# One core, a delta-rule recurrence and a GELU MLP: the written order of all five instruction queues is replaced by another

## The chip, the cores and the metric

The kernel runs on one core of a Trainium2 chip. The time is the device time of one execution in microseconds (us), the median of three runs. The core has five engines that the text names as the profile does: PE (matrix products; PEld is its weight load), DVE, ACT and POOL (elementwise work), and SP, which here only issues DMA transfers. Each engine works off its own queue in order.

## The reference

Four batches of eight heads run a delta-rule recurrence over 768 tokens with a 48 x 48 state; its output, 3072 tokens of 384 numbers, goes through an MLP with the tanh form of GELU.

```python
k_n = k / (np.linalg.norm(k, axis=-1, keepdims=True) + 1e-06)
for t in range(S):
    y[:, :, t] = np.einsum('bhd,bhde->bhe', q[:, :, t], state)
    v_old = np.einsum('bhde,bhd->bhe', state, kt)
    state = state + bt[:, :, :, None] * np.einsum('bhd,bhe->bhde', kt, vt - v_old)
...
h = x @ w_in
g = 0.5 * h * (1.0 + np.tanh(c * (h + 0.044715 * h * h * h)))
return g @ w_out
```

Here B, H, S, D are 4, 8, 768, 48, w_in is 384 x 2048 and w_out 2048 x 384. Inputs and output are float32; the kernel's products are in bfloat16.

## The kernel before

The 768 steps are cut into 12 chunks of 64 tokens. A chunk has 32 heads in all (batch and head); they are worked on as two units of 16 heads, so there are 24 units: chunk c has the units 2c and 2c+1. Two heads share the 128 partitions. Within a chunk the recurrence is solved as a triangular system, so that only a 48 x 48 state passes from chunk to chunk.

The names in the order are operation, dot, chunk or unit. For a chunk c: k, q, v load it (four DMA issues each; the k of chunk 0 comes in two halves, k0x0 and k0x1, of four issues each). sq, sum, pow, eps, inv make 1/norm of k. For a unit u: kn and qb write normalized k and q in bfloat16 (tile tok); T (for the first four units Tk and Tq) transposes them on PE and kT (kTk, kTq) copies them out of PSUM, or one DMA, turn, does both; G (GD, GQ) are the products of k with k and with q; dn copies the first and wq masks the second on DVE, or wqa on ACT with wqb on POOL. vb casts v.

For a chunk, leaf: F folds dn, lp multiplies by beta, x0 begins a recursion inside blocks of 8 tokens, L spreads lp, and twelve short DVE steps xm1, xa1 to xm6, xa6 run the recursion, each on the one before. xb multiplies by beta. For a unit: xe spreads xb into a tile zt of 128 x 1024, KZ is a product with it, kz its copy, GM two products, lw their masked copy (128 x 1024), and X10, X11 build the start of the inverse in tile bd. Two rounds refine it: A4, rt4, B4, then two copies into bd (bde40 and bde41 straight from PSUM, or xi4 on ACT or DVE and bdc40, bdc41 on POOL or DVE), and the same with 5 for 4.

For a chunk, chain: V and K form the right side from v and the state, R copies it, U solves with bd, Un copies, S makes the state's step and Sn adds it, Q and O make the output, On copies it, X with xT (or one DMA, turnx) transposes it. The MLP of a chunk is sixteen up products of three matmuls (up0 to up15, 128 x 256, line 780), four gelu on ACT of 1024 columns (line 784), eight down products of four matmuls (down00 to down13, 128 x 384, line 791), two copies Z0, Z1 and the output's DMA. Every chunk's MLP needs its own chain, and every chain needs the state of the chunk before; everything ahead of V does not.

At the start there are presets: constants by memset, copy and affine select on DVE and POOL (ident, sel, rows, blk, own, mlw, muq, tmpl and others; bdz, pad, tri and ladj preset tiles that are later only partly written), beta's load, transposes (betaT) and spreading (betaS, betaC), and warm_up (line 419), products of a zero tile wz with itself, 128 x 512, whose results nobody reads.

The weights W1 (w_in) and W2 (w_out) come in two transfers each (w1.0, w1.1, w2.0, w2.1 at lines 477 and 479), issued on POOL's queue. w1 waits for the loads of k of chunk 1, w2 for those of v of chunk 0.

No scheduler runs when the kernel is built. ORDER is one long text, found beforehand, with each operation's engine (a ACT, d DVE, g POOL, s SP, none PE) and, after an @, its PSUM bank of eight. Flow.order puts the operations into the five queues in this order and checks that each stands behind what it needs; Flow.emit adds the semaphore waits. An operation that ORDER leaves out is not done: so it picks between the two ways of a choice (turn or T, wq or wqa and wqb, xi with bdc or bde, turnx or X) and how many zero products run. POOL's work on the upper 64 partitions waits for that on the lower and the other way about. Where a wait stands, the whole queue behind it stands too; DMA issues wait in the same queue as the engine's other work.

## Time and profile before

| | us |
|---|---|
| three runs | 262.83, 263.09, 263.68 |
| median | 263.09 |
| the profiled execution, its own time | 262.76 |
| its span, first to last instruction | 261.0 |

The span is what the profile's rows add up to; the profiled execution's own time is 1.8 us above it. In rows of a timeline the first number is the start and the second the length, both in us from the span's start; in brackets stands the engine's idle time just before and what ended it. Rows of the busy time by stage begin with the stage. SPq, POOLq and ACTq are DMA issues. In the chain of waits each row is a start, a length and what the end of the program waited for at that time. PEclk is the granted clock as a share of full speed. The DMA share is the mean busy share of 16 DMA engines and can pass 1 where packets overlap. In the page's last part the last number is the median us from a DMA's issue to its landing.

### The profile page before, as it was taken

The numbers are of one execution on the slowest core, as the hardware profiler recorded it, in microseconds if no ns is written. First come the engines' busy times: TensorE is split into PE (matmuls) and PEld (weight loads), VectorE is DVE, ScalarE is ACT, GpSimd is POOL, SyncE is SP. The second block draws the span as 40 slices with busy tenths as digits, with TensorE's granted clock in tenths as the row PEclk, the third lists the DMA queues.
The fourth block names the chain that finished last, engine by engine and source line by source line (L and its number), as shares of the span: only waits on it lengthen the run. The fifth ranks groups of instructions, "written<-read, shape, count | busy, mean of one in ns | idle before, by whom it ended". The sixth has DMA issues, their size and how long they took to land.

```text
span 261.0 us, 11939 instructions
## 1 busy us (share of the span) xinstructions
PE 236.6 (91%) x5320; PEld 182.3 (70%) x5320; DVE 191.2 (73%) x444; ACT 169.5 (65%) x261; POOL 135.7 (52%) x172
## 2 busy tenths in 40 slices
...
GB/s 97 162 173 197 123 148 199 127 128 141 133 114 144 124 153 57 122 125 110 162 119 140 108 36 118 159 37 135 130 76 3 4 154 32 31 36 48 45 93 60
DMA packets 104019, 28.10 MB, mean 108 GB/s; under 512 B 98080, under 2 KB 103200, under 8 KB 103968
## 3 DMA queue, kind: packets, MB, share of 16 engines
q1 hardware_dynamic: 98736, 23.56, 51.4%
...
q10 hardware_dynamic: 2352, 0.64, 1.3%
...
HBM read 20.64 MB, written 4.72 MB: 97 GB/s over the span
## 4 chain that ended last, share of the span: by engine, by line
PE 62%; DVE 12%; DMA 10%; SPq 6%; POOL 4%; ACT 3%; issue 2%; POOLq 0%
PE ps L780 20%; PE ps L791 20%; DMA qraw<-in_q_dram 8%; SPq L468 6%; PE ps L660 6%; DVE lw L600 2%; PE ps L597 2%; PE ps L586 2%; PE ps L708 2%; PE ps L546 2%; DMA kraw<-in_k_dram 2%; PE ps L610 1%; PE ps L729 1%; PE ps L522 1%; PE ps L715 1%
## 5 line engine op out<-in xcount | busy, mean ns | idle before, releaser
L780 PE MATMUL ps<-xT,W 128*128 128x256 bf16 x576 | 75.6, 274 | 1.6 <-issue 0.8
L791 PE MATMUL ps<-W,gT 128*128 128x384 bf16 x384 | 72.3, 326 | 0.0
L784 ACT ACTIVATE gT<-ps 128x1024 bf16<-128x1024 f32 x48 | 48.3, 1020 | 22.0 <-PE ps L780 21.7
L780 PEld LDWEIGHTS ps<-xT,W 128*128 128x128 bf16 x576 | 51.7, 98 | 10.7 <-issue 1.2
L791 PEld LDWEIGHTS ps<-W,gT 128*128 128x128 bf16 x384 | 34.1, 97 | 18.6
L678 POOL COPY bd<-xi 64x256 f32<-64x256 f32 x28 | 11.0, 398 | 49.3 <-ACT xi L341 43.5
L600 DVE CAST_PREDICATED lw<-mlw,ps 128x1024 bf16<-128x1024 uint16 x24 | 29.1, 1218 | 7.6 <-PE ps L597 7.4
L650 POOL TENSOR_SCALAR_AFFINE_SELECT bd<-lw 64x512 bf16<-64x512 bf16 x33 | 22.3, 678 | 21.4 <-DVE lw L600 16.0
L494 POOL TENSOR_TENSOR nrm<-nrm,half 128x16 f32<-128x16 f32 x10 | 29.4, 2943 | 4.5 <-DVE nrm L492 4.3
L666 DVE TENSOR_TENSOR rl<-ps,two 128x384 bf16<-128x384 f32 (+1 forms) x48 | 22.8, 486 | 10.6 <-PE ps L660 10.4
L660 PE MATMUL ps<-rl,bd 128*128 128x64 bf16 x384 | 19.5, 198 | 0.7 <-DVE rl L666 0.7
L344 ACT ACTIVATE bd<-ps,low 128x512 bf16<-128x512 f32 x27 | 18.3, 677 | 2.3 <-DVE bd L341 2.3
L341 ACT ACTIVATE bd<-ps 64x512 bf16<-64x512 f32 x27 | 15.7, 585 | 5.9 <-PE ps L660 5.7
L632 DVE TENSOR_TENSOR ps<-ps,xl 128x96 f32<-128x96 f32 (+2 forms) x72 | 16.0, 223 | 4.0 <-PE ps L626 2.1
L660 PEld LDWEIGHTS ps<-rl,bd 128*128 128x128 bf16 x384 | 16.4, 101 | 3.1 <-DVE rl L666 0.9
L522 PE MATMUL ps<-ident,tok 128*128 128x128 bf16 x96 | 10.1, 256 | 8.9 <-POOL tok L513 6.7
L341 DVE COPY ob<-ps 128x384 f32<-128x384 f32 x7 | 3.9, 551 | 19.0 <-PE ps L791 19.0
L660 PEld LDWEIGHTS ps<-lw,bd 128*128 128x128 bf16 x384 | 15.1, 98 | 3.7 <-ACT bd L344 0.5
L635 DVE TENSOR_TENSOR xl<-ps,xl 128x96 bf16<-128x96 f32 (+2 forms) x72 | 16.2, 225 | 1.8
L660 PE MATMUL ps<-lw,bd 128*128 128x32 bf16 (+1 forms) x384 | 17.1, 183 | 0.3 <-ACT bd L344 0.3
L513 POOL TENSOR_TENSOR tok<-kraw,nrm 128x384 bf16<-128x384 f32 x16 | 14.6, 914 | 3.3 <-DVE xl L635 1.1
L341 ACT ACTIVATE dn<-ps 128x512 bf16<-128x512 f32 x20 | 11.9, 594 | 5.7 <-PE ps L546 5.5
(125 smaller groups left out, 437.3 us busy)
## 6 DMA issues: line engine op xcount, KB each, us to landing
...
W<-in_moe_w_in_dram POOLq DMA_DIRECT2D x2, 768.0 KB, 10.5
W<-in_moe_w_out_dram POOLq DMA_DIRECT2D x2, 768.0 KB, 10.8
kraw<-in_k_dram ACTq DMA_DIRECT2D x5, 48.0 KB, 3.3
kT<-tok SPq DMA_TRANSPOSE x12, 3.3
```

The costliest lines, as they stand in the source:

```text
L341: return e.activation(out, in_, ACT.Copy) if e is nc.scalar else e.tensor_copy(out, in_)
L344: return e.activation(out, in_, ACT.Copy, scale=by) if e is nc.scalar else e.tensor_scalar(out, in_, by, None, op0=ALU.mult)
L494: if e is nc.scalar else e.tensor_tensor(nr[:, 1, hx], nr[:, 0, hx], half[:, hx], ALU.pow), reads=[nrn, "half"] + ["one"] * (c < ROOTS),
L600: A(("dve",), op("lw"), lambda e, P: e.copy_predicated(lw[m][:, :, :, :].rearrange("p h w t -> p h (w t)"), mlw[:, :, :].rearrange("p w t ...
L632: A(("dve",), f"xm{m}.{c}", lambda e, P, m=m, w=w, part=part: e.tensor_tensor(part(P), P(f"L.{c}")[:, off[m]:off[m] + 2 * H * w].rearrange ...
L635: A(("dve",), f"xa{m}.{c}", lambda e, P, m=m, part=part: e.tensor_tensor(xl[y][:, :, m + 1:LB], part(P), xl[y][:, :, m + 1:LB], ALU.add), ...
L650: A(("pool", "dve"), op(f"X1{a}"), lambda e, P, src=lw[m][hf(a), :, 1, :], dst=bd[b_][hf(a), :, hf(a)], a=a: e.affine_select(out=dst, in_= ...
L660: ins = e.matmul(P(name)[:, C * h + c0:C * h + c1], bd[b_][:, h, :], rhs[:, h, c0:c1])
L666: A(("dve",), op(f"rt{i}"), lambda e, P, i=i, c0=c0, c1=c1, r_=r_: e.tensor_tensor(r_[:, :, c0:c1], P(ps(f"A{i}")).rearrange("p (h t) -> p ...
L780: ins = e.matmul(P(ph)[:, 256 * f:256 * f + 256].rearrange("p (x t) -> p x t", x=2), W1[:, j, 128 * (i + f):128 * (i + f) + 128], x_[:, :, ...
L784: A(("act",), f"gelu{i // 4}.{c}", lambda e, P, i=i, ph=ph: e.activation(g_[:, i:i + 4, :], P(ph).rearrange("p (f t) -> p f t", f=4), ACT. ...
L791: ins = e.matmul(P(po)[:, 0:DM], g_[:, f, 128 * b:128 * b + 128], W2[:, f, :], start=(f == 0), stop=(f == FC - 1))
```

## The change

ORDER is replaced as a whole, and with it the place of all operations, the engine of many, the PSUM banks, and some choices. The operations' code stays; only the number of zero products that exist to be chosen from goes from 70 to 140. All line numbers move by one (line 780 becomes 781).

What differs between the two orders by count: zero products 8 and 17, the 17 spread in ones and twos over the first 350 of 1668 entries; sel, ident, wz, four of the six bdz and some pads on POOL instead of DVE; k0 loaded wholly by ACT's queue, and beta's part partly by SP's, where k1 now comes first; q0, q1 and q2 issued ahead of v0; the W1 transfers behind the first kn and qb on POOL; the recursions of chunk 0 and 1 woven into each other; transposes of kn and qb by DMA 14 instead of 12, of the output 8 instead of 10; wqa with wqb 12 instead of 10; qb 13 on ACT and 7 on POOL instead of 8 and 12; vb 4 on ACT, 8 on DVE, 12 on POOL instead of 10, 4, 10; X11 12 on DVE and 12 on POOL instead of 4 and 20; X10 8 and 16 instead of 11 and 13; xb 10 on DVE instead of 6. In the new order KZ.4, KZ.5, GM.4, GM.5, A5.3 and B4.3 stand ahead of the first up product, in the old one behind it.

The two orders up to where the first up products stand:

```diff
 ORDER = """
-ident:d tmplz:d tmpl0:g one:g blk1:g tmpl1:g triwq4:g pad4:d wz:d bdz5:d blk2:g ident2:g bdz4:g k0x0.11:s k0x1.10:s k0x0.10:a k0x0.00:a k0x0.01:a
-k1.11:s k0x1.11:s k0x1.00:a k0x1.01:a k1.01:s k1.00:s k1.10:s beta01:a tabS:a beta00:a blk3:g pad5:d ladj5.0:d pad1:d mmlw:d bdz2:d identf:d two:d
-rowz:d rows1:g mln0:g sq.0a:g triwq1:d unit:d bdz3:d ladj4.1:d own:d triwq2:d pad0:d sel:d ladj5.1:d sum.0a:d mwp0:g half:g pow.0a:a trilw2:d trilw3:d
-eps.0a:d inv.0a:d mmuq:d bdz1:g sq.0b:g k2.11:s k2.10:s k2.00:s beta11:a beta10:a kn.0:g fill0@0 fill1@0 fill2@0 fill3@0 fill4@0 fill5@0 fill6@0
-fill7@0 Tk.0@0 betaT0@1 sum.0b:d bdz0:d first1:d pow.0b:a eps.0b:d inv.0b:d kn.1:d Tk.1@2 sq.1:a sum.1:d kTk.0:a pow.1:a GD.0@4 kTk.1:d GD.1@2
-betaT1@0 k2.01:s dn.0:a dn.1:a sq.2:a F.0@2 betaN011:d eps.1:d pad3:d betaN010:d inv.1:d pad2:d betaN000:d betaN001:d kn.2:d kn.3:d sum.2:d Tk.2@3
-q0.01:s q2.00:s q0.00:s q0.10:s q0.11:s v0.00:s q2.10:s q2.11:s v0.10:s q2.01:s v0.11:s k3.10:s k3.01:s v2.10:s v0.01:s lp.0:d betaH0:d L.0@2 x0.0:d
-betaL0:d xm1.0:d betaN101:d xa1.0:d betaN110:d xm2.0:d betaN100:d xa2.0:d xm3.0:d xa3.0:d betaN111:d xm4.0:d Tk.3@1 trilw1:a triwq0:a kTk.2:a GD.2@4
-betaS0@3 kTk.3:a qb.0:a GD.3@6 Tq.0@1 dn.2:a qb.1:a Tq.1@0 betaC0:a dn.3:a betaH1:d xa4.0:d xm5.0:d xa5.0:d kTq.0:a ladj4.0:a kTq.1:a betaL1:d low1:d
-mln1:g w1.1:g trilw0:g first0:g w1.0:g pow.2:g eps.2:g betaS1@3 F.1@6 betaS3@7 xm6.0:d inv.2:d xa6.0:d xb.0:d xe.1:d KZ.1@2 kz.1:a qb.5:a lp.1:d L.1@6
-xe.0:d KZ.0@0 GM.1@4 x0.1:d xm1.1:d xa1.1:d xm2.1:d mwp1:g kn.5:g triwq5:g qb.4:g kn.4:g muq0:g muq1:g low2:g lw.1:d xa2.1:d T.5@2 kz.0:a betaC3:a
-kT.5:a betaC1:a GM.0@0 lw.0:d X10.1:g X11.1:g xm3.1:d xa3.1:d xm4.1:d xa4.1:d X11.0:g X10.0:g betaS2@7 G.5@4 T.4@2 GQ.0@0 A4.1@3 rt4.1:d B4.1@3
-q1.01:s k3.11:s k3.00:s q1.11:s q3.10:s q1.10:s q5.11:s q1.00:s q3.11:s k4.01:s v1.10:s k4.10:s v2.11:s q5.01:s v1.00:s v2.00:s v1.01:s q3.00:s
-k5.11:s v1.11:s k4.11:s k4.00:s q3.01:s dn.5:a betaC2:a wqa.5:a vb.1:a vb.0:a A4.0@7 xm5.1:d xa5.1:d kT.4:d xm6.1:d wq.0:d xa6.1:d rt4.0:d G.4@4
-bde40.1:a bde41.1:a dn.4:a sq.3:a A5.1@3 rt5.1:d B4.0@7 bde40.0:a bde41.0:a w2.1:g xb.1:g xe.3:d wq.4:d sum.3:d xe.2:g B5.1@3 V.0@0 KZ.3@2 F.2@6
-kz.3:a A5.0@7 R.0:a qb.2:a bde50.1:a bde51.1:a lp.2:d GM.3@4 L.2@6 x0.2:d rt5.0:d xm1.2:d xa1.2:d lw.3:d KZ.2@2 GQ.1@0 B5.0@7 xm2.2:d wq.1:d kz.2:a
-bde50.0:a bde51.0:a GM.2@2 w2.0:g pow.3:g eps.3:g xa2.2:d lw.2:d X11.2:g xm3.2:d X10.2:d xa3.2:d xm4.2:d inv.3:d xa4.2:d triwq3:d xm5.2:d xa5.2:d
-xm6.2:d Tq.2@4 U.0@0 qb.3:a kTq.2:a X10.3:g X11.3:g Un.0:a GQ.2@4 Tq.3@7 kTq.3:a O.0@0 On.0:a S.0@2 A4.2@7 Sn.0:a rt4.2:d xa6.2:d X.0@0 xb.2:g xe.5:g
-wq.2:d xT.0:a B4.2@7 GQ.3@2 A4.3@6 up8.0@0 up9.0 xe.4:d rt4.3:d tabG:a xi4.2:a KZ.4@4 kz.4:d B4.3@6 up10.0 up11.0 GM.4@4 wq.3:d lw.4:d X11.4:d
-...
+tmplz:g tmpl0:g one:d blk1:d tmpl1:g wz:g mmuq:g muq0:g mmlw:d pad0:g mln0:g ident:g ident2:g mwp0:g mln1:g bdz0:g triwq3:d bdz1:d ladj5.0:d mwp1:g
+pad3:g pad5:d trilw0:d pad1:d unit:d half:d blk2:g blk3:g rowz:d own:d muq1:g identf:d triwq0:g pad2:g k0x0.11:a k1.11:s k1.10:s beta10:s k0x1.01:a
+k0x1.00:a k0x1.11:a beta11:a q1.01:s q0.10:s k0x1.10:a q0.11:s k1.00:s k1.01:s k0x0.01:a k0x0.10:a q2.10:s k0x0.00:a k2.01:s q2.11:s sq.0b:g beta01:a
+beta00:a tabS:a fill60@0 betaT1@0 sum.0b:d pow.0b:a eps.0b:d sq.1:a inv.0b:d triwq5:d kn.1:d low1:d pad4:d sum.1:d sq.0a:a pow.1:a Tk.1@1 fill79@2
+betaN100:d betaN111:d sum.0a:d eps.1:d inv.1:d betaT0@2 pow.0a:a rows1:g sel:g q0.01:s q0.00:s k2.10:s k2.11:s q1.00:s k2.00:s betaN001:d eps.0a:d
+betaN110:d inv.0a:d betaN011:d betaN000:d betaN101:d betaN010:d betaH0:d q2.01:s q2.00:s kn.2:g Tk.2@3 qb.1:a kTk.2:a kTk.1:a sq.2:a ladj5.1:a kn.0:g
+Tk.0@2 GD.2@4 betaH1:d kn.3:d kTk.0:d dn.2:d bdz4:d Tk.3@3 Tq.1@2 qb.0:g GD.1@0 GD.0@4 betaL0:d sum.2:d betaL1:d dn.0:d kTk.3:a GD.3@6 Tq.0@3 dn.1:a
+dn.3:a F.1@6 F.0@7 kTq.0:d lp.1:d two:d betaS3@3 lp.0:d L.0@7 x0.0:d x0.1:d L.1@6 xm1.0:d xa1.0:d w1.1:g w1.0:g xm1.1:d xm2.0:d first1:g pow.2:g
+eps.2:g first0:g qb.4:g ladj4.0:a kTq.1:a xa2.0:d xa1.1:d xm3.0:d xm2.1:d inv.2:d xa2.1:d xa3.0:d xm3.1:d xm4.0:d xa3.1:d xa4.0:d xm5.0:d xa5.0:d
+betaS0@2 betaC0:a xm4.1:d xm6.0:d xa6.0:d xb.0:d xa4.1:d xm5.1:d xa5.1:d kn.4:g kn.5:g low2:g betaS1@4 qb.5:a betaC3:a triwq4:a q1.11:s v0.00:s
+v1.10:s v0.01:s q1.10:s fill126@5 T.4@5 fill32@3 betaC1:a triwq1:a ladj4.1:d xm6.1:d xa6.1:d xe.0:d xe.1:g xb.1:d kT.4:a v0.10:s v0.11:s fill115@4
+xe.3:d T.5@7 G.4@4 k3.11:s trilw1:a dn.4:a kT.5:a v1.00:s k4.01:s k3.00:s fill98@3 fill74@6 GQ.0@2 wq.0:d KZ.0@6 KZ.1@0 kz.1:a GM.1@0 k4.10:s q3.01:s
+KZ.3@7 fill16@2 xe.2:g lw.1:d X11.1:g triwq2:g qb.2:g kz.0:a q3.00:s G.5@2 wq.4:d trilw3:a kz.3:a dn.5:a qb.3:a tabG:a wqa.5:a GM.0@0 GM.3@6 lw.0:d
+F.2@4 lp.2:d X10.1:d betaS2@5 fill38@0 KZ.2@4 A4.1@0 kz.2:a betaC2:a Tq.3@1 L.2@2 GM.2@4 kTq.3:a x0.2:d lw.3:d xm1.2:d vb.1:d X10.0:g k4.11:s v1.11:s
+k3.01:s k4.00:s q3.11:s k3.10:s bdz2:g X11.0:g vb.0:g trilw2:g A4.0@3 Tq.2@1 fill40@6 kTq.2:a fill127@6 bdz3:g X10.3:g X11.3:g wqb.5:g bdz5:g q3.10:s
+xa1.2:d rt4.1:d B4.1@0 bde40.1:a w2.1:g w2.0:g bde41.1:a xm2.2:d rt4.0:d xa2.2:d lw.2:d fill138@6 fill69@3 B4.0@3 A5.1@0 GQ.1@4 V.0@6 bde40.0:a
+bde41.0:a wqa.1:a A4.3@3 xm3.2:d xa3.2:d xm4.2:d rt5.1:d xa4.2:d xm5.2:d xa5.2:d rt4.3:d fill64@0 A5.0@4 B5.1@5 rt5.0:d xm6.2:d R.0:a bde50.1:a
+v1.01:s v2.00:s v2.01:s v2.11:s q4.01:s v2.10:s k5.01:s k5.10:s X11.2:d X10.2:d xa6.2:d xb.2:d xe.5:d wqb.1:g GQ.2@0 GQ.3@6 B5.0@4 bde51.1:a fill99@3
+wqa.3:a bde50.0:a bde51.0:a A4.2@5 B4.3@2 sq.3:a rt4.2:d xe.4:d KZ.5@3 U.0@6 fill73@5 Un.0:d sum.3:d B4.2@5 fill8@4 kz.5:a xi4.3:a bdc40.3:g bdc41.3:g
+GM.5@2 xi4.2:a bdc40.2:g O.0@6 KZ.4@5 A5.3@4 On.0:a wq.2:d rt5.3:d bdc41.2:d lw.5:d X.0@6 kz.4:a S.0@0 GM.4@4 vb.2:d lw.4:d X11.5:d pow.3:g eps.3:d
+vb.3:d xT.0:a Sn.0:a up8.0@6 up9.0 up10.0 up11.0 gelu2.0:a B5.3@0 up0.0@2 up1.0 up2.0 up3.0 A5.2@1 bde50.3:a qb.7:a gelu0.0:a V.1@6 X11.4:d X10.4:g
+A4.4@4 K.1 rt5.2:d rt4.4:d inv.3:d R.1:a bde51.3:a B5.2@1 bde50.2:d bde51.2:d X10.5:g A4.5@5 rt4.5:d kn.6:d qb.6:g wqb.3:g up4.0@2 B4.4@4 xi4.4:a
+bdc40.4:g up12.0@6 up5.0 up13.0 sq.4:a U.1@0 up14.0 up6.0 up7.0 T.6@5 Un.1:a gelu1.0:a kn.7:g bdc41.4:g Q.1@0 sum.4:d A5.4@4 kT.6:a rt5.4:d O.1 S.1@2
+B4.5@4 up15.0 On.1:d down00.0@5 down01.0 down02.0 gelu3.0:a bde40.5:a bde41.5:a B5.4@6 vb.4:g pow.4:g A5.5@4 down03.0 vb.5:d Sn.1:d rt5.5:d V.2@2
+B5.5@4 bde50.4:a bde51.4:a X.1@6 Z0.0:a xi5.5:a xT.1:d G.6@0 bdc51.5:g K.2 dn.6:a turn.7:s G.7@4 dn.7:a down10.0@6 q4.11:s q4.10:s F.3@7 R.2:a k5.00:s
+...
 """
...
         def warm_up():
-            for i in range(70):
+            for i in range(140):
                 n = f"fill{i}"
                 A(PE, n, lambda e, P, n=n: e.matmul(P(n), wz[:, 0:128], wz[:, :]), reads=["wz"], alloc=(n, 1), frees=[n], mode="m", mm=1)
```

139 lines of the change are left out of this document (67 added, 72 removed).

## The prediction

> **What bounds the kernel now.** I read the page first, then the busy time by stage, then TensorE's timeline and the chain of waits through the stage that is not full.
>
> ```profile
> span 261.0 us, 11939 instructions
> ...
> PE 236.6 (91%) x5320; PEld 182.3 (70%) x5320; DVE 191.2 (73%) x444; ACT 169.5 (65%) x261; POOL 135.7 (52%) x172
> ```
>
> ```profile
> 0.00:11.50 11.50, 3.59 (x8) 1.03 (x8) 10.33 (x30) 1.83 (x5) 9.15 (x21) 0.88 0.75 124
> 11.50:25.60 14.10, 11.78 (x192) 9.58 (x192) 12.71 (x48) 9.79 (x20) 8.39 (x11) 0.50 1.20 185
> 25.60:29.30 3.70, 2.08 (x94) 1.69 (x90) 2.35 (x6) 2.08 (x4) 1.91 (x6) 0.96 0.78 117
> 29.30:49.40 20.10, 16.89 (x403) 13.79 (x400) 16.73 (x42) 16.03 (x29) 13.42 (x16) 0.50 1.01 156
> ...
> 64.30:100.00 35.70, 35.70 (x977) 27.75 (x978) 33.70 (x86) 28.26 (x45) 26.82 (x27) 1.00 0.73 125
> 100.00:240.00 140.00, 137.66 (x3252) 106.79 (x3249) 104.59 (x221) 92.79 (x137) 66.45 (x84) 1.00 0.48 90
> 240.00:257.60 17.60, 17.55 (x132) 12.61 (x129) 0.56 (x1) 7.73 (x10) 0.00 (x0) 1.00 0.25 57
> 257.60:261.00 3.40, 0.00 (x0) 0.00 (x0) 0.00 (x0) 0.47 (x1) 0.00 (x0) 1.00 0.45 116
> ```
>
> The columns after the stage are its length, the busy time of PE, PE's weight loads, DVE, ACT and POOL, then granted clock, DMA share and GB/s. From 64.3 to 257.6 PE is busy 190.9 of 193.3 us: 2.4 us idle. The last 3.4 us are the output's way out. So a new order of the same work can gain only ahead of 64.3, where the clock is 0.50 for most of the time and DVE is busy 42.1 of the first 49.4 us (10.33 + 12.71 + 2.35 + 16.73). PE waits there for what DVE, POOL and the loads deliver.
>
> ```profile
> 11.81 0.61 PE L522 MATMUL ps<-ident,tok 128*128 128x128 bf16 x4 [6.68 <-POOL tok L513]
> ...
> 49.10 1.12 PE L780 MATMUL ps<-xT,W 128*128 128x256 bf16 x6
> ...
> 57.77 0.62 PE L597 MATMUL ps<-kT 48*64 48x64 bf16 x32 [1.58 <-ACT xi L341]
> ...
> 64.28 0.44 PE L738 MATMUL ps<-us,tok 64*64 64x48 bf16 x32 [1.97 <-DVE us L341]
> ```
>
> ```profile
> 14.70 12.50 DMA qraw<-in_q_dram
> 27.25 0.51 POOL tok L341
> ...
> 32.61 8.09 DMA qraw<-in_q_dram
> 40.72 0.52 ACT tok L341
> ```
>
> Two loads of q, issued behind the two transfers of W1 and the first of W2, land 12.5 and 8.1 us after issue, and a cast stands waiting for each. The MLP's first product starts at 49.10.
>
> **The change, part by part.** Loads first. Before, SP stands 4 us in one issue once a weight transfer is under way:
>
> ```profile
> 14.70 4.01 SPq L468 DMA_DIRECT2D qraw<-in_q_dram  x1
> ```
>
> ```profile
> 4.18 2.06 POOL L380 TENSOR_SCALAR_AFFINE_SELECT rows<-rows 128x1024 bf16<-128x1024 bf16 x1
> ...
> 6.54 0.82 POOL L491 TENSOR_TENSOR sq<-kraw 128x384 f32<-128x384 f32 x1
> ...
> 12.07 1.01 POOL L477 DMA_DIRECT2D W<-in_moe_w_in_dram  x1
> ...
> 13.83 0.80 POOL L477 DMA_DIRECT2D W<-in_moe_w_in_dram  x1
> ...
> 35.02 1.91 POOL L579 TENSOR_TENSOR zt<-xb,blk 128x1024 bf16<-128x1024 bf16 x1
> ```
>
> After, W1 stands on POOL behind sq.0b, rows1, sel, kn.2, kn.0 and qb.0. sq.0b needs the second half of k0, whose last piece is the sixth on ACT's queue: five issues take 3.7 us, so it is issued near 5 and, at 3.3 us from issue to landing (both rows in the next fences), lands at 8.3. Then 0.82 + 2.06 + 1.9 for sel (no POOL row; the product of that size, 1.91) brings 13.1; with the wait for 1/norm, kn.2, kn.0 and qb.0 end near 16.4. W1 leaves at about 16.4 and 17.4 instead of 12.07 and 13.83. By then SP, at 0.68 us a piece, has issued all of q0, q2 and half of q1: the two waits of the chain go. W1 landed 10.5 us after its issue, so by 28 here, over twenty before its use, beside the front of chunk 0 and 1, which covers it: moving it costs nothing. First transposes: sq 0.82, sum 0.54, root 0.21, eps 0.16, 1/x 0.20, kn 0.56 after 8.3 give 11.3 with waits: as before (11.81).
>
> ```profile
> 0.81 3.70 ACTq L468 DMA_DIRECT2D kraw<-in_k_dram  x5
> ```
>
> ```profile
> L632 DVE TENSOR_TENSOR ps<-ps,xl 128x96 f32<-128x96 f32 (+2 forms) x72 | 16.0, 223 | 4.0 <-PE ps L626 2.1
> ...
> W<-in_moe_w_in_dram POOLq DMA_DIRECT2D x2, 768.0 KB, 10.5
> W<-in_moe_w_out_dram POOLq DMA_DIRECT2D x2, 768.0 KB, 10.8
> kraw<-in_k_dram ACTq DMA_DIRECT2D x5, 48.0 KB, 3.3
> ```
>
> ```profile
> 2.14 0.23 DVE L414 TENSOR_SCALAR rl<-tmpl 128x256 bf16<-128x256 bf16 x1
> ...
> 4.72 1.57 DVE L414 TENSOR_SCALAR rl<-tmpl 128x128 bf16<-128x128 bf16 x1
> 4.77 1.53 DVE L388 TENSOR_TENSOR own<-blk 128x64 bf16<-128x64 bf16 x1
> ...
> 22.28 0.29 DVE L637 TENSOR_TENSOR xb<-xl,bc 128x128 bf16<-128x128 bf16 x1
> ...
> 35.38 2.10 DVE L579 TENSOR_TENSOR zt<-xb,blk 128x1024 bf16<-128x1024 bf16 x1
> ...
> 43.53 1.22 DVE L600 CAST_PREDICATED lw<-mlw,ps 128x1024 bf16<-128x1024 uint16 x1 [0.62 <-PE ps L597]
> ```
>
> ```profile
> 43.89 0.82 PE L729 MATMUL ps<-rs,bd 128*128 128x48 bf16 x16
> ```
>
> Second, chunk 0's front becomes later and chunk 1's earlier. Both 8x8 recursions are now woven on DVE. Their folds F.1 and F.0 stand behind all four dn copies and end near 22 (from kn.0 at 15.9: transpose 0.6, copy 0.4 to 0.6, dn 0.7, sum 0.9, memset 0.5, second dn, two folds of 0.9). From about 23.2, twenty steps of 0.22 and their issue bring xb.0 at 28.6, where it was at 22.6; eight more instructions bring xb.1 at 31, where it was near 35 (on POOL). Six us lost for chunk 0, four won for chunk 1.
>
> Third, from there to the first solve U.0 (before 43.89). xe.3 on DVE stands beside xe.2 on POOL as before, and took 2.10 there; then wq.0 0.68, lw.1 1.22, wq.4 0.68 and lw.0 1.22 come in line, and X10.1, which frees the whole inversion of unit 1, stands behind lw.0: 37.3. A4.1, another lw 1.22, rt4.1, B4.1, two bd copies on ACT, A5.1, rt5.1 and the like for unit 0 end at rt5.0 near 45.7; R.0 and two pairs of bd copies later U.0 starts at 49.0. From U.0 to the first product it was 5.2 us (43.89 to 49.10), so 54.2, with PE at half clock all the way. A lower bound is DVE's own work: the instructions ahead of rt5.0, each at the median of its kind, sum to 41.0 us against 40.3 before, when it began at 39.6. With the 4.6 us that DVE must wait at the start and for the folds, and 2.7 off for own and a preset, which took 1.5 us each beside POOL's rows1 before (a preset twice as large took 0.23 with POOL elsewhere) and stand beside shorter POOL work now, rt5.0 is at 42.4 and the first product at 50.9.
>
> Fourth, 17 zero products, no longer eight in a row at the start but in ones and twos among the real ones, all ahead of the first up product. Eight took 3.59 us at half clock, so nine more are 4.0 us, or 2 us at full clock; they are in the walk to 54.2 where they stand on its way (two ahead of B4.1, two ahead of B4.0, one ahead of A5.0).
>
> ```profile
> 1.54 3.59 PE L422 MATMUL ps<-wz 128*128 128x512 bf16 x8 [1.54 <-DVE wz L353]
> ```
>
> ```profile
> 26.00:27.00 1.00, 0.26 (x32) 0.15 (x20) 0.85 (x2) 0.00 (x0) 0.00 (x0) 1.00 1.00 144
> 27.00:28.00 1.00, 0.12 (x3) 0.15 (x4) 0.77 (x2) 0.79 (x2) 0.75 (x2) 1.00 0.76 127
> ...
> 29.00:30.00 1.00, 0.79 (x28) 0.64 (x27) 1.00 (x1) 1.00 (x2) 0.84 (x3) 0.63 0.55 99
> ```
>
> Before, the clock rose at 25.6 at the end of a full stretch, and fell at 29.3 after two microseconds with 0.38 us of work. In the new order five zero products stand ahead of GQ.0 and KZ.0, about 24 to 30, where DVE runs the recursions and PE would stand still. If they hold a full clock from 25 on, the products on the way from 30 to 49 (GM, A4, B4, A5, B5, V, U and zero products between them, 9 us cold) shrink by 4.5. I take half, 2.2 us: first product at 52.0, 2.9 later than before, between 50 (full clock, DVE's bound) and 54.2. [...]
>
> Fifth, what is left at the first product. Ahead of it now stand KZ.4, KZ.5, GM.4, GM.5, A5.3 and B4.3 too, 1.8 us warm by start to start (0.35, 0.35, 0.33, 0.33, 0.20, 0.23); with PE's pace in the full stages that is 1.9 us less to do: −1.9. The two holes after it, 1.58 and 1.97 us, are chunk 1's inversion and us being late; chunk 1 is ahead now (DVE's work up to rt4.3 sums to 40.5 instead of 49.6), and Un.1 is on ACT. ACT's line there (xT.0, Sn.0, gelu2 1.02, bde50.3, qb.7, gelu0 1.02, R.1, bde51.3) ends 6.0 us after xT.0 begins to write, and PE has 6.2 us of products until U.1: little is left over. I take 1 us of holes instead of 3.55: −2.5. W2 now waits on POOL until about 44.5 and 45.5 (32.09 and 36.87 before); with 10.8 us to landing it is there at 56.3, and the first down product comes 10 us after the first up, at 62. That cover is 5.7 us; if W2 takes longer, PE stops for the excess.
>
> Sixth, the rest: the same groups, two PE transposes that become DMA transposes on SP less two that come back, so PE's work is equal within 0.3 us. I leave the 2.4 us of holes as they are, with −1 to +3 as bounds, since every instruction of the full stage has a new neighbour. The tail is unchanged in kind: last products, one ACT copy, two outputs: 3.40.
>
> Sum: +2.9 − 1.9 − 2.5 = −1.5 us. The profiled execution took 262.76 (span 261.0); the runs' median is 263.09. Forecast: 261.2 us, its own range 259 to 263.
>
> **The rivals.** One, the clock stays up from 25 on. For it: five zero products just where PE would stand still. Against it: the fall at 29.3 above. First product at 50, so 2 us less than the forecast, and no holes after it, another 1: 258.2, with 256.5 to 259.5 as bounds.
>
> Two, chunk 0's lateness comes through, the slower side. Place: X10.1 on DVE behind lw.0, everything behind it cold, zero products in PE's line ahead of B4.1 and B4.0. First product at 54.2 or later (+5.1), −1.9, and holes of the old size return because us and xi are again late against a full PE: +3.2, 266.0. It decides the sign when the first product comes later than 51.0 plus the holes saved: with 2.5 saved, after 53.5. For it: DVE was nearly full before, and its waits at the start are now real ones. Against it: the port's 2.7 us and the q loads.
>
> Three, nothing nets: the six us that chunk 0 loses and the four that chunk 1 wins cancel, within 0.3% of 263.09, so 262.3 to 263.9.
>
> **How the numbers follow.** Forecast 0.41 (of it four fifths below 262.3), rival one 0.17, rival two 0.28, rival three 0.14. Faster by over 0.3%: 0.17 + 0.34 = 0.51, 0.53 with rival three's edge; within 0.3%, which a measurement of this kernel hardly tells from nothing: 0.17; slower: 0.30. The range takes in rival one's middle and rival two: 256.8 to 266.5. A longer hole of the full stage (+3) on rival two would end above it, and is left out.
>
> **What would show it.** First L780 product: 52 means the sum holds, 50 rival one, 54 and later rival two. The granted clock between 25 and 49 tells these two apart. No wait for qraw over 1 us before 45. The two holes of 1.58 and 1.97 gone. DVE's xb at 28 to 29 in chunk 0. PE idle from 64 to the end at 2 to 3 us. It is wrong if PE waits for W2, or if the full stage shows over 5 us of holes.

## The result, and the profile after

| | before | after |
|---|---|---|
| median of 4 runs each, us | 262.96 (262.66 to 263.68) | 269.74 (269.23 to 272.13) |
| ratio, 95% interval | | 1.027 (1.021 to 1.034) |
| the profiled execution, its span | 262.76, 261.0 | 269.23, 267.4 |

The change made the kernel 6.8 us slower; 261.2 was predicted, with 266.5 as the upper end. The page of the changed kernel begins:

```profile
span 267.4 us, 11922 instructions
...
PE 230.6 (86%) x5318; PEld 176.4 (66%) x5325; DVE 202.7 (76%) x455; ACT 166.1 (62%) x258; POOL 136.7 (51%) x167
```

DVE is 11.5 us busier (202.7 against 191.2). Some of that is work that came over from POOL (455 instructions instead of 444); some 6 us of it is overrun: over the whole execution DVE's instructions exceeded the usual time of their kind by 11.7 us before and by 17.5 after (my sums over the two traces). The busy time by stage of the changed kernel (columns as before: length, PE, weight loads, DVE, ACT, POOL, clock, DMA share, GB/s):

```profile
11.50:25.60 14.10, 8.03 (x149) 6.12 (x150) 13.26 (x38) 5.91 (x14) 9.48 (x9) 1.00 1.15 155
25.60:29.30 3.70, 1.86 (x40) 1.45 (x39) 3.50 (x22) 3.21 (x7) 2.83 (x8) 1.00 1.11 202
29.30:49.40 20.10, 13.12 (x425) 10.00 (x428) 19.29 (x41) 17.26 (x30) 15.49 (x18) 0.97 0.70 118
49.40:64.30 14.90, 11.96 (x328) 10.15 (x327) 13.90 (x21) 10.62 (x17) 9.21 (x11) 0.93 0.73 108
64.30:93.00 28.70, 28.57 (x739) 22.04 (x740) 23.01 (x57) 24.74 (x39) 15.95 (x15) 1.00 0.67 121
93.00:106.00 13.00, 9.55 (x242) 6.88 (x238) 10.28 (x25) 7.83 (x13) 7.39 (x9) 1.00 0.59 112
106.00:257.60 151.60, 149.25 (x3368) 114.57 (x3366) 114.39 (x241) 91.73 (x136) 67.93 (x76) 1.00 0.52 93
```

The record of the clock begins at 24 us here; ahead of it 1.00 only means that there is none. One row has no counterpart before: 93 to 106, with PE busy 9.55 of 13 us. The same stretch of the kernel before:

```profile
93.00:106.00 13.00, 12.96 (x348) 10.46 (x348) 12.56 (x28) 10.89 (x17) 11.84 (x10) 1.00 0.62 103
```

348 products there, 242 after. To see how far the changed kernel is behind at each point, I gave each of PE's operations its usual time at full clock, and compared when the same amount of this work is left to do. The times are my sums, not rows of a view; another way of pricing the products moves what is lost between two rows by up to 1 us:

| PE's work left, us | before, at | after, at | behind |
|---|---|---|---|
| 192 (first up products) | 52.3 | 54.7 | 2.4 |
| 184 | 64.6 | 65.5 | 0.9 |
| 160 | 89.6 | 90.7 | 1.1 |
| 150 | 100.0 | 106.0 | 5.9 |
| 50 | 206.2 | 212.9 | 6.7 |
| 2 | 255.1 | 261.4 | 6.3 |

So the head costs about 1 us, the stretch from 93 to 106 costs 4.8, and the rest half a microsecond. Of the 4.8, idle time of PE accounts for 3.45 (13.00 less 9.55). Where PE stood still, from the timeline of the changed kernel (its lines are one higher than before):

```profile
14.51 0.61 PE L523 MATMUL ps<-ident,tok 128*128 128x128 bf16 x4 [4.85 <-DVE low L395]
...
54.34 0.83 PE L781 MATMUL ps<-xT,W 128*128 128x256 bf16 x6 [0.27 <-ACT xT L342]
...
58.54 0.56 PE L716 MATMUL ps<-vb,zt 128*128 128x48 bf16 x16 [0.98 <-DVE vb L342]
59.84 0.36 PE L661 MATMUL ps<-lw,bd 128*128 128x48 bf16 x8 [0.73 <-DVE bd L653]
...
97.88 0.41 PE L587 MATMUL ps<-zt,tok 128*64 128x128 bf16 x8 [0.80 <-DVE ps L633]
...
99.74 0.56 PE L730 MATMUL ps<-rs,bd 128*128 128x48 bf16 x16 [0.69 <-DVE xl L636]
...
101.37 0.44 PE L752 MATMUL ps<-us,wq 64*64 64x48 bf16 x32
101.64 0.32 PE L739 MATMUL ps<-us,tok 64*64 64x48 bf16 x18
103.77 0.30 PE L739 MATMUL ps<-us,tok 64*64 64x48 bf16 x14 [1.81 <-issue]
```

The waits at 14.51, 97.88 and 99.74 end with DVE. The one at 103.77 is of another kind: it lies inside one operation (S.3, 18 of its 32 small products done), and the profile names nothing that PE waits for: PE and DVE are idle, while ACT is busy for 1.44 of the 1.79 us from 101.97 on and POOL ends an instruction. For the waits on DVE, its rows stand beside POOL's:

```profile
10.86 1.12 DVE L497 TENSOR_SCALAR nrm<-nrm 128x8 f32<-128x8 f32 x1 [0.28 <-ACT nrm L494]
...
12.13 1.85 DVE L342 COPY wq<-tmpl 128x512 bf16<-128x512 bf16 x1
...
94.79 0.92 DVE L638 TENSOR_TENSOR xb<-xl,bc 128x128 bf16<-128x128 bf16 x1
...
96.06 1.67 DVE L580 TENSOR_TENSOR zt<-xb,blk 128x1024 bf16<-128x1024 bf16 x1
...
9.95 2.01 POOL L381 TENSOR_SCALAR_AFFINE_SELECT rows<-rows 128x1024 bf16<-128x1024 bf16 x1
11.92 1.92 POOL L390 TENSOR_TENSOR sel<-ident,own 128x1024 bf16<-128x1024 bf16 x1
...
94.40 1.16 POOL L569 TENSOR_TENSOR wq<-wq,muq 128x512 bf16<-128x512 bf16 x1
...
96.04 1.15 POOL L569 TENSOR_TENSOR wq<-wq,muq 128x512 bf16<-128x512 bf16 x1
```

eps.0b, eight numbers a partition, ends with rows1; the preset triwq5 with sel; xb.4 and xe.8 overrun beside wqb.7 and wqb.11. All of them stand in line ahead of what PE waits for. I call this the port theory: some DVE instructions take longer beside one of POOL's (eps.0b took 1.12 us here and ended at 11.98, rows1 at 11.96; it took 0.17 in e1_early below, where rows1 was moved away). The name is mine: the rows show times, and nothing that the two engines share. The hole inside S.3 suggested a second, the refill theory: that PE runs out of instructions. That is my reading of these rows: a transfer of 16,384 bytes on the queue that the profile names instruction ran there from 101.11 to 102.45; there are 42 of these in the execution, about one for every 253 of PE's 10,643 products and weight loads, and PE went on 1.32 us after this one had landed.

### The profile page after: what moved, and what is told of

Same layout as the page of the kernel before. It is cut to its first block, busy times and chain, and to the rows that moved or that the text cites. A ratio compares the mean times of both kernels' runs of the same rounds, so it can differ in the third digit from the quotient of the medians.

```text
span 267.4 us, 11922 instructions
## 1 busy us (share of the span) xinstructions
PE 230.6 (86%) x5318; PEld 176.4 (66%) x5325; DVE 202.7 (76%) x455; ACT 166.1 (62%) x258; POOL 136.7 (51%) x167
## 3 DMA queue, kind: packets, MB, share of 16 engines
HBM read 20.64 MB, written 4.72 MB: 95 GB/s over the span
## 4 chain that ended last, share of the span: by engine, by line
PE 69%; DVE 22%; issue 3%; POOL 3%; ACT 2%; POOLq 0%
PE ps L792 21%; PE ps L781 20%; PE ps L661 7%; DVE lw L601 3%; PE ps L587 3%; PE ps L598 3%; PE ps L547 2%; PE ps L611 2%; PE ps L709 2%; DVE xl L636 2%; DVE rl L667 2%; DVE ps L633 2%; DVE zt L580 2%; DVE bd L653 2%; PE ps L730 2%
## 5 line engine op out<-in xcount | busy, mean ns | idle before, releaser
L781 PEld LDWEIGHTS ps<-xT,W 128*128 128x128 bf16 x576 | 51.5, 97 | 9.9 <-DVE st L746 1.0
L495 POOL TENSOR_TENSOR nrm<-nrm,half 128x16 f32<-128x16 f32 x10 | 29.9, 2988 | 11.5 <-DVE nrm L493 11.4
L651 POOL TENSOR_SCALAR_AFFINE_SELECT bd<-lw 64x512 bf16<-64x512 bf16 x28 | 19.2, 689 | 23.5 <-DVE lw L601 16.8
L580 POOL TENSOR_TENSOR zt<-xb,blk 128x1024 bf16<-128x1024 bf16 x9 | 18.1, 2024 | 8.8 <-DVE xb L638 8.7
L514 POOL TENSOR_TENSOR tok<-kraw,nrm 128x384 bf16<-128x384 f32 x16 | 13.2, 830 | 13.4 <-PE ps L739 7.6
L661 PEld LDWEIGHTS ps<-lw,bd 128*128 128x128 bf16 x384 | 13.8, 96 | 6.3 <-ACT bd L342 1.6
L633 DVE TENSOR_TENSOR ps<-ps,xl 128x96 f32<-128x96 f32 (+4 forms) x72 | 15.4, 220 | 2.9 <-PE ps L627 1.5
L636 DVE TENSOR_TENSOR xl<-ps,xl 128x96 bf16<-128x96 f32 (+4 forms) x72 | 15.9, 227 | 1.8
L523 PE MATMUL ps<-ident,tok 128*128 128x128 bf16 x80 | 7.9, 246 | 9.8 <-DVE low L395 4.8
L342 ACT ACTIVATE bd<-ps 64x512 bf16<-64x512 f32 x23 | 13.3, 585 | 4.1 <-PE ps L661 3.9
L345 ACT ACTIVATE bd<-ps,low 128x512 bf16<-128x512 f32 x23 | 15.3, 676 | 0.4 <-DVE bd L342 0.4
L342 ACT ACTIVATE ob<-ps 128x384 f32<-128x384 f32 x19 | 9.3, 489 | 10.1 <-PE ps L792 9.7
```

Source lines behind the costliest of these rows:

```text
L342: return e.activation(out, in_, ACT.Copy) if e is nc.scalar else e.tensor_copy(out, in_)
L495: if e is nc.scalar else e.tensor_tensor(nr[:, 1, hx], nr[:, 0, hx], half[:, hx], ALU.pow), reads=[nrn, "half"] + ["one"] * (c < ROOTS),
L580: A(("dve", "pool"), op("xe"), lambda e, P: e.tensor_tensor(zt[m][:, :, :].rearrange("p h (b j) -> p h b j", j=LB), xb[y][:, H * x:H * x + ...
L633: A(("dve",), f"xm{m}.{c}", lambda e, P, m=m, w=w, part=part: e.tensor_tensor(part(P), P(f"L.{c}")[:, off[m]:off[m] + 2 * H * w].rearrange ...
L636: A(("dve",), f"xa{m}.{c}", lambda e, P, m=m, part=part: e.tensor_tensor(xl[y][:, :, m + 1:LB], part(P), xl[y][:, :, m + 1:LB], ALU.add), ...
L651: A(("pool", "dve"), op(f"X1{a}"), lambda e, P, src=lw[m][hf(a), :, 1, :], dst=bd[b_][hf(a), :, hf(a)], a=a: e.affine_select(out=dst, in_= ...
```

## The experiments

All are edits of ORDER; ratios are to the kernel before on the same chip. The runs were made on different chips, on which the kernel before had medians from 261.10 to 262.76 us, so medians of different rows are compared by their ratios. "Lost" is what is lost between 160 and 150 us of work left, as in the table above. Holes are those over 0.3 us inside one operation of PE, after 24 us.

| run | median | ratio (95%) | span | first transposes | U.0 | first up | lost | holes |
|---|---|---|---|---|---|---|---|---|
| r1_same | 268.77 | 1.024 (1.017 to 1.030) | 268.0 | 14.33 | 50.10 | 55.75 | 3.9 | 0.48, 1.62 |
| e1_early | 268.16 | 1.021 (1.011 to 1.031) | 262.4 | 13.51 | 47.71 | 52.98 | 1.7 | none |
| e2_wqb | 267.45 | 1.019 (1.010 to 1.028) | 264.1 | 14.55 | 49.51 | 54.93 | 1.0 | none |
| e3_burst | 268.51 | 1.023 (1.016 to 1.030) | 267.3 | 14.39 | 48.67 | 54.43 | 3.7 | 0.82, 0.89 |
| e5_ab | 265.66 | 1.018 (1.014 to 1.022) | 263.6 | 13.52 | 48.75 | 54.90 | 1.0 | 1.09 |
| e6_abg | 264.62 | 1.013 (1.009 to 1.017) | 262.2 | 13.52 | 48.12 | 53.77 | 0.9 | 1.06 |
| e4_nozero | 269.98 | 1.034 (1.028 to 1.039) | 267.8 | 14.33 | 50.23 | 56.92 | 2.8 | 1.28 |
| e7_block | 265.39 | 1.012 (1.008 to 1.015) | 266.1 | 13.51 | 47.22 | 52.57 | 4.3 | 1.80, 2.04 |
| e8_shift | 270.23 | 1.030 (1.025 to 1.034) | 269.0 | 14.40 | 50.16 | 56.51 | 2.2 | 1.04, 0.57 |
| e9_again | 265.81 | 1.012 (1.007 to 1.017) | 263.5 | 13.54 | 48.16 | 54.35 | 1.0 | 1.58 |
| e10_seven | 267.33 | 1.015 (1.006 to 1.023) | 265.6 | 13.54 | 47.46 | 53.06 | 2.6 | 1.62, 0.41, 1.01, 0.88 |

**The changed kernel again** (r1_same), with no edit.

> The changed kernel once more, as the measure for the runs beside it. All theories: ratio near 1.027, first up product near 54.3, PE's holes at 97.1 (0.80), 99.1 (0.69) and 102.0 (1.81) in the same places. If the 1.81 us hole, for which the trace names no releaser, is chance, it is elsewhere or gone.

The hole inside S.3 is there again (1.62 us), eps.0b and triwq5 are as long as before (1.12 and 1.85), and x0.5 (1.15). But the waits of 0.80 and 0.69 for DVE are not there, against the expectation:

```profile
93.00:106.00 13.00, 11.15 (x284) 8.01 (x273) 10.96 (x30) 9.32 (x15) 8.95 (x10) 0.96 0.68 126
```

POOL's vb.8 waits 1.37 us for its load here, and wqb.7 runs at 96.91 instead of 94.40: xb.4 takes 0.29, xe.8 0.86, and xe.9 1.40 beside wqb.11, without PE having to wait. So which DVE instruction is hit, and whether PE waits for it, differs between executions of one program. The head differs too, by a microsecond. Here the clock is at a half from 33.3 to 40.1, in the first profile it is full from 24.2 to 48.1. The first solve's right side, V.0, starts at 44.57 instead of 42.73, and U.0 at 50.10 instead of 49.06.

**Presets out of the way** (e1_early):

```diff
-identf:d triwq0:g
+identf:d sel:d ladj4.1:d triwq0:g
...
-q2.11:s sq.0b:g
+q2.11:s rows1:g sq.0b:g
...
-pow.0a:a rows1:g sel:g q0.01:s
+pow.0a:a q0.01:s
...
-triwq1:a ladj4.1:d xm6.1:d
+triwq1:a xm6.1:d
```

> Three presets moved out of the way: rows1 on POOL ahead of sq.0b instead of behind it, sel on DVE in its idle time before 9 us instead of on POOL beside the norms, and the preset ladj4.1 there too instead of inside the recursions. [...] Order theory (the weaving of the two recursions and the products set ahead of U.0 cost the time, the standing DVE instructions are covered): first up product within 0.7 us of 54.3, end within 0.7.

```profile
12.42 0.17 DVE L497 TENSOR_SCALAR nrm<-nrm 128x8 f32<-128x8 f32 x1 [0.28 <-ACT nrm L494]
...
12.74 0.24 DVE L342 COPY wq<-tmpl 128x512 bf16<-128x512 bf16 x1
...
13.51 0.61 PE L523 MATMUL ps<-ident,tok 128*128 128x128 bf16 x4 [4.37 <-DVE low L395]
```

eps.0b 0.17 instead of 1.12, triwq5 0.24 instead of 1.85. From these overruns of the first profile, as an estimate, I had expected the transposes at 12.3, the first up product at 51.5 to 52.5 and the end 1 to 2.5 us earlier. The transposes come only 1.0 us earlier, because rows1 now stands ahead of sq.0b; U.0 follows by 1.35 us. The first up product, 52.98, is just outside its range. The span fell by 5.0 us, twice what I had expected at most: no hole over 0.3 us stood in this execution. The median hardly moved: two executions took 264.29 and 267.42, the other two 268.89 and 272.12.

**The wqb products out of the way** (e2_wqb):

```diff
-kn.9:g
+kn.9:g wqb.6:g wqb.7:g
...
-wqb.6:g eps.6:g
+eps.6:g
...
-wqb.7:g vb.9:g
+vb.9:g
...
-wqb.11:g xe.10:g
+xe.10:g wqb.11:g
```

> The POOL products wqb.6 and wqb.7 moved ahead of pow.5 (POOL idle near 75), wqb.11 behind xe.10. Port theory: between 92 and 97 the recursion's x0.5 (1.15 us), xb.4 (0.92) and xe.8 (1.67) fall to 0.33, 0.29 and 0.69, PE's holes of 0.80 and 0.69 close and the end comes 2 to 3 us earlier. Order theory: DVE has too much in line there anyway, the holes stay within 0.3 us and the end within 0.7. Refill theory (PE's hole of 1.81 is an instruction refill that comes too late for a run of small products): that hole stays within 0.5 us, near S.3.

```profile
94.71 0.29 DVE L638 TENSOR_TENSOR xb<-xl,bc 128x128 bf16<-128x128 bf16 x1
...
95.36 0.68 DVE L580 TENSOR_TENSOR zt<-xb,blk 128x1024 bf16<-128x1024 bf16 x1
```

```profile
93.00:106.00 13.00, 13.00 (x345) 10.01 (x341) 11.61 (x31) 10.92 (x18) 6.80 (x9) 1.00 0.82 130
```

xb.4 at 0.29 instead of 0.92, xe.8 at 0.68 instead of 1.67 (x0.5 0.33 instead of 1.15), and PE does 345 products from 93 to 106 without a pause. The port theory is right on the instructions: x0.5 takes 0.33 us in all six profiles in which wqb.6 was moved and 1.15 in all six of the new order in which it was not. That the waits of PE closed shows less, since they were also absent from r1_same and e1_early, where no wqb was moved. The hole in S.3 went too; the refill theory had expected it to stay, and this run does not explain it. The median does not show the gain by itself: 1.019 against 1.024 in the repeat, with intervals that overlap.

**Two up products between O.3 and S.3** (e3_burst):

```diff
-O.3 S.3@0 Sn.3:d On.3:a sq.7:a up14.2 up15.2
+O.3 up14.2 up15.2 S.3@0 Sn.3:d On.3:a sq.7:a
```

> Two up products (0.66 us of PE, 12 instructions with their weight loads) moved from behind S.3 to between O.3 and S.3. Refill theory: PE now gets through the same instructions more slowly, the hole of 1.81 inside S.3 shrinks by 0.6 to 1.8 us and the end comes 0.5 to 1.5 us earlier. Rival (the hole is something else, a lost wait on another engine): the hole stays at 1.8 and S.3, Sn.3 and the end come up to 0.7 us later.

The hole in S.3 shrank to 0.82 us, as the refill theory had it, and another of 0.89 appeared at 111.8: the end came no earlier.

**Both moves** (e5_ab: e1_early and e2_wqb together), **and two collisions of the head** (e6_abg: also wqb.5 behind vb.4, and eps.3:d to eps.3:g behind pow.3).

> The moves of the second and third run together: rows1, sel and ladj4.1 early, wqb.6 and wqb.7 behind kn.9, wqb.11 behind xe.10; TensorE's order unchanged. [...] First transposes at 11.9 to 12.5 instead of 14.51, first up product at 52 to 53.3 instead of 54.3 to 55.4, x0.5, xb.4 and xe.8 below 0.8 us each, the holes of 0.80, 0.69 and 1.81 us between 97 and 104 below 0.3 us in sum, profiled span 260.5 to 262.5 (the two runs alone had 262.4 and 264.1). Refill theory (TensorE runs dry of instructions wherever small products come dense, whatever VectorE does): a hole of over 0.8 us with all engines idle inside the S or O products near 97 to 104 stays, span 263 to 266. If chance decides (runs of one kernel have lain from 264.3 to 272.1): the median stays within 1 us of 268.

> As the run before, and two collisions of the head mended as well: wqb.5 behind vb.4 on GpSimd, so that wqb.1 (1.2 us) is over before xb.2 (0.99 us beside it, 0.27 alone) and X11.2 starts beside a shorter rest of W2's issue; eps.3 on GpSimd behind pow.3 instead of VectorE (1.61 us there, 0.15 alone). Port theory: xb.2 at 0.3 us and U.0 some 0.6 us earlier, first up product at 51.5 to 52.7; V.1 one us earlier (eps.3 out of VectorE's queue), so that the hole ahead of K.1 shrinks; span 259 to 261, that is 1 to 2 us below the run before it and at or below the kernel before (261.3). Rival: the lane of the weight copies and gelu is what holds the up products of chunk 0, so that V.1 earlier changes nothing: span within 0.5 us of the run before it.

The excess over the kernel before falls from 6.0 us in the repeat to 4.6 and 3.5, each against the kernel before on its own chip, and the executions lie closer (263.72 to 265.36 in the second). In the first the waits at 97 to 104 went, as expected, but the first up product (54.90 for 52 to 53.3) and the span (263.6 for 260.5 to 262.5) missed: a hole of 1.09 us stood in S.0. The second span, 262.2, missed its 259 to 261. Why eps.3 on POOL did not help is in its rows of DVE and POOL:

```profile
55.59 1.79 DVE L342 CAST vb<-vraw 128x384 bf16<-128x384 f32 x1
57.41 1.26 DVE L653 TENSOR_TENSOR bd<-lw,two 64x512 bf16<-64x512 bf16 x1
...
55.26 1.45 POOL L651 TENSOR_SCALAR_AFFINE_SELECT bd<-lw 64x512 bf16<-64x512 bf16 x2 [1.21 <-DVE lw L601]
56.67 0.49 POOL L342 CAST tok<-qraw 128x384 bf16<-128x384 f32 x1
57.15 1.24 POOL L569 TENSOR_TENSOR wq<-wq,muq 128x512 bf16<-128x512 bf16 x1
```

vb.3, now first in line, stands through three POOL instructions that follow one another without a pause (X10.4, X10.5 and qb.6; in e7_block, with the two X10 gone from POOL, it takes 0.36 us), as eps.3 did before it (1.61 us at 56.52 in the changed kernel): here mending one passed the wait on.

**No zero products** (e4_nozero: the 17 entries fill60 to fill8 left out).

> The changed kernel without its 17 zero products; nothing else is altered. If the clock decided the head (rival one of the prediction), the granted clock stays at a half up to 49 or later, the dense products from 29 on take twice as long and the first up product comes 1.5 us or more later: span 269 to 272. If VectorE's lateness decides it (port theory), the first up product stays within 0.7 us of 54.3 to 55.4 although the clock is lower, and the span stays within 1 us of 268; what TensorE does before 49 is then covered by waits.

```profile
25.60:29.30 3.70, 1.86 (x31) 1.64 (x28) 3.49 (x22) 2.96 (x7) 2.93 (x7) 0.75 1.12 201
29.30:49.40 20.10, 15.05 (x403) 12.61 (x401) 18.20 (x39) 17.14 (x29) 14.79 (x18) 0.58 0.70 115
```

With the clock at 0.58 instead of 0.97 up to 49, U.0 starts at 50.23. In the five profiles with the same head (the changed kernel, its repeat, e2_wqb, e3_burst, e8_shift), at 0.83 to 0.97, it starts between 48.67 and 50.16. The first up product is at 56.92, of which 1.28 is a hole in S.0: without it 1.3 later than in the first profile, and 0.1 earlier than in the repeat. The span (267.8) is the port theory's. The first up product by its number is the clock rival's, and less the hole the port theory's (53.6 to 56.1). So this run alone does not decide between them. With the waits for DVE at 100 and 102 unchanged (0.80 and 0.69), there was no hole in S.3.

**The block at 55 to 58** (e7_block: e6_abg with X10.4 and X10.5 on DVE behind X11.4, wqb.3 behind kn.7), **and the same kernel a second time** (e9_again).

> As the run with rows1, wqb.5 and eps.3 moved, and the block of GpSimd instructions at 55 to 58 us taken from beside VectorE's work: X10.4 and X10.5 on VectorE behind X11.4, wqb.3 behind kn.7. In the run before it vb.3 stood 1.79 us (0.35 alone) and X11.4 1.26 us (0.41 alone) beside X10.4, X10.5, qb.6 and wqb.3, which follow one another on GpSimd without a pause. Port theory: vb.3 at 0.35 to 0.5, X11.4 at 0.4 to 0.6 us, the two X10 cost VectorE 0.8 us in all, so V.1 and the blocks of chunk pair four come 1 to 1.5 us earlier; the wait ahead of K.1 (about 1 us at 58) goes; span 260.5 to 261.7 against 262.2, median 263 to 264. Rival: up products and gelu of chunk 0 hold TensorE there; the span stays at 262 to 262.5.

> The kernel of the run with the block at 55 to 58 us mended, once more. Its profiled execution had 266.1 us, two holes of 1.80 and 2.04 us inside K.1 and S.3 and half a clock for 3.4 us behind the second; five of its other six executions had spans of 263.0 to 263.7. Refill theory: a hole inside an operation always ends 1.28 to 1.46 us after a transfer of TensorE's instructions has landed, and whether a transfer meets a run of small products differs between executions of one kernel; this profile has other holes than the last, and its span is 266.1 less (plus) what they take less (more). Rival: the holes are tied to the kernel and stand again in K.1 and S.3, within 0.4 us of their sizes.

vb.3 took 0.36 us, X11.4 and the two X10 1.21 together, V.1 came 2.4 us earlier, and nothing was won: medians 265.39 and 265.81 (1.012 both times, 1.013 in e6_abg), against an expected 263 to 264. PE's timeline of the first, then of the second, shows where it went:

```profile
58.52 0.41 PE L709 MATMUL ps<-st,kT 48*64 48x48 bf16 x28 [1.80 <-issue]
...
99.08 0.32 PE L739 MATMUL ps<-us,tok 64*64 64x48 bf16 x19
101.44 0.28 PE L739 MATMUL ps<-us,tok 64*64 64x48 bf16 x13 [2.04 <-issue]
```

```profile
53.41 0.57 PE L739 MATMUL ps<-us,tok 64*64 64x48 bf16 x27 [1.58 <-issue]
...
99.74 0.46 PE L739 MATMUL ps<-us,tok 64*64 64x48 bf16 x32
```

Holes of 1.80 in K.1 and 2.04 in S.3 in one execution; none in either place and 1.58 in S.0 in the other. The same program, so the holes are not tied to an operation: the refill theory's expectation. The second span is 2.6 us shorter, its holes 2.3. Behind the hole in S.3 the clock was at a half from 102.3 to 105.7; in the second execution it was not.

**The program shifted**: 14 more zero products in the changed kernel (e8_shift), seven in e7_block's (e10_seven), all where PE waits for beta or for the first k.

```diff
-fill60@0 betaT1@0
+fill60@0 fill0@6 fill1@6 fill2@6 fill3@6 fill4@6 fill5@6 fill6@6 fill7@6 betaT1@0 fill9@6 fill10@6 fill11@6 fill12@6 fill13@6 fill14@6
```

> The changed kernel with 14 more zero products at the start, 8 ahead of betaT1 and 6 behind it, where TensorE has nothing else to do (from 2.5 to 8.0 and from 9.4 to 14.2 us). [...] Refill theory: the hole of 1.81 us (1.62 in the repeat) inside S.3 goes or moves elsewhere, as it went in the run without zero products (moved the other way by 27 instructions); what is lost between 93 and 106 us falls from 4.8 to 2.8 to 3.3 us; span 265 to 266.5. If the hole belongs to the waits before it and not to where the program stands, it stays at 1.5 to 1.9 us inside S.3, and the span at 267.5 to 268.5.

> The same kernel with seven more zero products ahead of betaT1 (2.5 to 8 us, where TensorE waits for beta), which only shift where its program stands against the pieces in which it is fetched. Refill theory: the holes inside operations stand elsewhere or are gone, each again 1.2 to 1.5 us behind a landed piece; without any the span is 261 to 262.5, with one more of 1 to 2 us it is 263 to 264.5. Rival: holes in K.1 and S.3 as before.

In e8_shift the hole left S.3 (lost: 2.2 us instead of 4.8 and 3.9), and others came in A5.3 and O.4, with one of 0.78 us at 107.72 between two operations, which the table does not count; in e10_seven they lie in A4.4, Q.3, S.3 and O.4. Neither was faster: both shifted kernels still had holes. The span of 265 to 266.5 expected of e8_shift was missed (269.0); its clock fell once more, from 57.0 to 60.4.

**The kernel before, profiled once more** (e11_before; one execution, 263.57, span 261.8).

> The kernel before, profiled once more. Its first profile had one hole inside an operation after 24 us (0.60 us at 131.4), the profiles of the changed kernel and its variants one to four of 0.4 to 2.0 us each, two none. If the old order is spared because its small products stand apart, the sum of such holes stays below 1 us here and the span at 259 to 262; if it only had luck in that one profile, holes of 1 us or more appear, each 1.25 to 1.5 us behind a landed transfer of instructions.

No hole over 0.3 us inside an operation. But the old order is not free of them: two small ones (0.23 in O.0, 0.28 at 132.75) are there, and between two operations PE stands 0.71 us until 117.49, with nothing named and 1.52 us after a transfer of instructions has landed. Over 0.3 us inside operations the two profiles of the old order have 0.60 us together; of the twelve of the new order and its variants, ten have 1.1 to 3.9 us each, two have none. Two profiles are few to tell the orders apart by. No version here beats the kernel before; the nearest is e7_block with 1.012.

## Why the prediction was wrong

Two things failed. In the sum, the full stage was given its old 2.4 us of holes, and it cost 5.4 us more than before. In the head, the gain from the clock was taken back by DVE instructions that stood beside POOL's work, which the sum had at nothing.

**Right.** The place of X10.1 (37.18 for 37.3), no wait for a load of q over 1 us, none for W2, the two old holes of 1.58 and 1.97 gone.

**Right by luck.** xb.0 came at 28.83 for 28.6, but its steps began at 24.78 for 23.2 and took 4.1 us for 5.4. U.0 came at 49.06, the time that the walk gave for half a clock, with the clock full up to 48.1.

**First step, "First transposes ... 11.3".** They came at 14.51. sq.0b ran 0.9 us after the time that I gave it (9.17 for 8.3), and the rest is eps.0b and triwq5 beside rows1 and sel. The sum had sel on POOL and its price there, but not what stands on DVE beside it. e1_early took 1.0 us of it back.

**Third step, "2.7 off for own and a preset".** I counted as a gain that two old collisions ended (1.57 and 1.53 us beside rows1). The two run side by side, from 4.72 to 6.29 in the kernel before, so that some 1.4 us was to be won and not 2.7, and new ones came in their place, on the path (first step). This term is not in the sum: it made the lower bound of 50.9 and spoke against rival two.

**Fourth step, the clock, "I take half, 2.2 us".** The clock did stay up, from 24 to 48, as rival one had it (before, its rise was at 25.9, not 25.6). Up to V.0 it was worth about 1.5 us: r1_same, the same program at half clock from 33.3 to 40.1, has xb.1 0.29 us later and V.0 1.84 later.

```profile
42.73 0.58 PE L716 MATMUL ps<-vb,zt 128*128 128x48 bf16 x16
...
48.49 0.64 PE L587 MATMUL ps<-zt,tok 128*64 128x128 bf16 x8 [1.21 <-DVE zt L580]
49.06 0.82 PE L730 MATMUL ps<-rs,bd 128*128 128x48 bf16 x16
...
44.84 1.70 DVE L653 TENSOR_TENSOR bd<-lw,two 64x512 bf16<-64x512 bf16 x2
...
46.72 0.99 DVE L638 TENSOR_TENSOR xb<-xl,bc 128x128 bf16<-128x128 bf16 x1
47.74 0.69 DVE L580 TENSOR_TENSOR zt<-xb,blk 128x1024 bf16<-128x1024 bf16 x1
```

Behind V.0 it was lost again. U.0 stands in PE's queue behind KZ.5, KZ.5 waits for xe.5 on DVE, and in line ahead of xe.5 X11.2 took 1.25 us beside the issues of W2 (the first of the two in the row at 44.84) and xb.2 0.99 beside wqb.1: 1.5 us over their 0.42 and 0.29. The sum had no such term. Then the clock fell to a half from 48.1 to 51.5, and from U.0 to the first up product it was 5.3 us. That is as long as before, at half clock throughout (5.2); e6_abg and e9_again, with the clock full for all but the last 0.9 and 1.5 us, took 4.6 without their hole. So about 0.7 us was lost there, and with the 1.5 this is, as an estimate, 2.2 of the 2.3 us between the forecast's 52.0 and the measured 54.34. That is rival two's time, by another way than rival two's: it had everything behind X10.1 cold. The 2.3 us are nearly all of the 2.4 by which the head was missed.

**Fifth step.** −1.9 for work already done was −2.8 (5.2 behind by time at the first up product, 2.4 by work). −2.5 for holes was −1.5 (2.4 behind, then 0.9): 0.98 and 0.73 remained, both waits for DVE beside POOL (eps.3, X11.4). Together as predicted. The head came out at +0.9 instead of −1.5.

**Sixth step, "I leave the 2.4 us of holes as they are, with −1 to +3".** Here lies the larger part: the rest cost 5.4 us. From 64.3 to its last product PE was idle 6.0 us, where it had been 2.3 before. In 93 to 106 it was idle 3.45: 0.80 and 0.69 behind the overruns beside wqb.6, wqb.7 and wqb.11, and 1.81 in S.3. That these DVE instructions are longer beside POOL's is shown (e2_wqb: xb.4 0.29 us for 0.92, xe.8 0.68 for 1.67); that PE waits for them is so in this execution and not in r1_same, which has the hole alone, 4.3 us of idle time from 64.3 on, and is as slow. The hole's cause is not shown by an edit of its own; what speaks for it is below. In the first profile that leaves, with the head's 0.9, about 2 of the 6.4 us of span in which PE was busy. In 93 to 106 alone, 0.9 to 1.0 us are lost by my table in the runs without a hole or an overrun there (e2_wqb, e5_ab, e6_abg, e9_again), although PE is busy for all 13.00 us in them. Whether the products took longer or I priced them too low stays open. I had bounded the stage by the sum of the old holes and +3, without asking which new neighbours DVE and POOL get in it.

**The rivals.** Two had the time of the first up product (54.2 or later), and expected holes after it that did not come in that size; its 266.0 was short because no case had the full stage in it.

On the overruns, xe.8 took 1.67 us beside wqb.11 (1.15), and 0.68 in e2_wqb, where POOL's first cast of vb began 0.31 us after it. Which instruction of POOL stands beside each one of DVE would have been the question to put to each neighbour in the new order.
